# Batch 1's order of work dealt anew in a single-core attention and SwiGLU kernel

## The chip, the core and the metric

The kernel runs on one core of a Trainium2 chip. Its engines run side by side, each through its own list of instructions in order: TensorE (PE in the profile) multiplies matrices, VectorE (DVE) and GpSimd (POOL) do elementwise work, ScalarE (ACT) copies and takes exponentials, SyncE (SP) issues DMA transfers; ACT issues some transfers too. Semaphores make an instruction wait for what it needs. The metric is the device time of the one core in microseconds, start to end, so lower is better.

## What is computed

Eight batches, each of 8 heads with 512 tokens and 32 states of 64 elements. Tokens read from the states and the states read from the tokens, and both results go through one SwiGLU layer with a norm ahead of it:

```python
scores  = softmax(scale * x @ state.T)    ; xread = scores @ state
scores2 = softmax(scale * state @ x.T)    ; sread = scores2 @ x
y  = concat([xread, sread], axis=2)       # (8, 8, 544, 64) -> 4352 rows of 512
xn = y / sqrt(mean(y*y) + 1e-6) * rms_g
g  = xn @ w_gate                          # 512 -> 1536
out = (g * sigmoid(g) * (xn @ w_val)) @ w_out
```

All of it is in float32.

## The kernel before

The weights are converted and stored in DRAM during batch 0. Batches 1 to 7 then run one body each (lines 1288 to 1306), which builds some 17 "streams": Python generators, each of which issues one small step when it is called. A string of letters, written out by hand or by a planner, says whose step comes next. Batch 1 has a string of its own, `FIRST` (line 37), batches 2 to 6 use `PERIOD` and batch 7 uses `LAST`. The schedule is manual: each engine, and each queue of transfers, works in the string's order. A step's data dependencies follow from the program; a buffer that is still in use makes its next owner wait until it is given back.

The streams of batch 1, with the names used below:

- `h`: 42 products on PE (line 806) for six pairs of hidden columns. Pair n has x1, z1, x2, z2, y, x3 and x4, so "h5.z2" is one step. Two products of the next pair come ahead of x4. x, y and z are PSUM banks; x has two buffers, y and z one.
- `t`: per pair three ACT copies out of x, z and x again, and the SiLU (lines 853 to 860). `u`: per pair the DVE sums g1 += z, g0 += y, c += x, then fin1 and fin0 (line 882), which multiply gate and value into the hidden tile `hb`; pairs 3 to 5 have two more (lines 888 and 894).
- `v`, `x`, `w`: folding the states into the gate and value weights. `v` and `w` are products on PE (line 659), called v2 to v5 for this batch and w0, w1 for the next; `x` copies them (ACT, line 671) and forms their four sums (POOL, lines 686 to 689).
- `p`: 49 products on PE (line 1109) in seven groups p0 to p6 of seven steps each ("p3.3" is the fourth step of group 3), the two-level fast multiplication with `w_out`. `k`: the DVE sums that these need. q0.0 to q6.3 (lines 1157 to 1163) are four quarter sums for each group, "half" (line 1168) changes `hb` in place, "add" (line 1149) adds a bank to a kept copy. `c` copies the banks out (ACT, line 1119). `o` stores the output.
- `q`: only in batch 1: the quarter sums of `w_out` on POOL (line 1063), W0 to W6, four steps each, and their store to DRAM (`t_d<-w`, line 1065). `G` and `g` fetch them again from there for each use (`w<-t_d`, line 1055). The tile `w` has three buffers for all of these.
- `f` fetches weights (`w_m<-w_d`, 1 MB each, line 194), `l` loads the state and x of batch 3.
- `a`: what the tokens of batch 2 read: transpose of the states, four transposes `xB` of x, a transfer to DRAM and four back (`xG`, on ACT's queue, lines 378 and 383), the scores (PE, line 403), softmax on DVE and ACT, two transposes into `aT_s` (line 503), the reads (PE, line 530), squares (ACT, line 537), the norm (lines 452 to 469) and the scaling of `aT_s` by it (line 544).
- `s`: what the states of batch 2 read: two maxima, exponentials (line 564), their block transpose `eB` (DVE, line 582), a transfer to DRAM (line 585) and four back into `e` (line 589), both on ACT's queue; then the state read (PE, line 600), which multiplies these transposed exponentials with x, its scaling (line 611), a transpose (line 615) and a copy (line 617).

The lines where the transposed exponentials leave and return:

```python
nc.scalar.dma_start(out=e_d[b % 2].rearrange(...), in_=eB.rearrange(...))
for g in range(4):
    nc.scalar.dma_start(out=e2T[Ns * g:Ns * g + Ns].rearrange(...),
                        in_=e_d[b % 2][:, :, g].rearrange("j t f -> t j f"))
```

Lines 659 to 1005 hold several functions which all write PSUM tiles named `at`, `pv` and `f`: `at` and `pv` have two buffers each.

Of the kernel before, what the change touches and what calls it, by code (L numbers as in the profile page):

```python
# [34 lines left out]
)  # L35

FIRST = (
    "vxhthhthhthuxuufththaaaaaqfhhqthahtqqquuuuxavvhuhhxxtuthuhthtuhuhuaqhvfxxxtuqqqx"
    "tqhqqqqhutkqqhqtaahauhuGGhutuhhhutGuuhtthhhxxuuxtqqquaaauaahhhthagthhthsuuuuuuhp"
    "ppkpptukupuqqqqkkppukkkkkppaakkkggkcacppppppppcappppssaaakplqapkkkkkpkkkppppaaak"  # L40
    "ccaasapppssakscfqaaaapqkkappkkkakppppakkosasqksappppskssgglsaoooapspppakkkaooafw"
    "wxsxxpgcpcowxoxfxg"
)
LAST = (
    "vxhhffththhtuhhhavuttuuhhtfuhhgxxthhhuuuxxtuthuhtthuhuxhutuvxxxvhthhutkxghhtuhut"
# [1299 lines left out]
```

## Time and profile before

| what | us |
|---|---|
| runs | 762.13, 758.90, 762.27 (median 762.13) |
| the profiled execution | 759.87 |
| its span in the trace | 758.1 |
| PE busy in the span | 745.8 (98%) |
| DVE busy | 597.9 (79%) |
| ACT busy | 350.4 (46%) |
| POOL busy | 293.9 (39%) |
| all DMA queues | 146.17 MB, mean 193 GB/s |

The profiled execution's own time is 1.77 us above its span: what lies ahead of the first and behind the last instruction. "Busy" counts time in which the engine had an instruction running. An engine near 100% can still lose time when its instructions run slower than elsewhere, so the stretches of one batch are best compared with those of another that runs the same instructions. Batch 1 runs from about 131 us to 221 us in the trace, batches 2, 3 and 4 follow at about 80 us each.

### The profile page before, as it was taken

What the parts mean: (1) busy time and instruction counts of PE and PEld (TensorE: products, weight loads), DVE (VectorE), ACT (ScalarE), POOL (GpSimd) and SP (SyncE); (2) the same over time, 40 slices, a digit from 0 to 9 for tenths busy, and PEclk for the clock granted to TensorE, in tenths of its full rate; (3) what the DMA queues carried; (4) which work ended last, traced back from release to release, by engine and by line L of the source; (5) the groups of instructions that cost most, each with busy time, mean ns of one, the idle gap of its engine ahead of it and who ended that gap; (6) DMA issues with size and microseconds to landing.
All of it is one profiled execution on the core that took longest, in us unless ns stands there. A gap on an engine that the chain in (4) does not pass through costs nothing.

```text
span 758.1 us, 14411 instructions
## 1 busy us (share of the span) xinstructions
PE 745.8 (98%) x5641; PEld 596.5 (79%) x5641; DVE 597.9 (79%) x1000; ACT 350.4 (46%) x548; POOL 293.9 (39%) x379
## 2 busy tenths in 40 slices
PE   9999999999889999999999999999999999999998
PEld 7633444779768898879877997799788987899997
DVE  4999997679937997689948994799579965787961
ACT  5989883552235522643255425543456236411220
POOL 2000004992574326532465129312842275323600
PEclk9999999999999999999999999999999999999999
DMA  9887945773866176725684477517661866132311
GB/s 297 263 265 264 346 170 181 272 249 112 270 199 236 35 292 201 287 56 196 245 280 115 161 245 244 185 65 301 216 224 26 304 204 216 53 103 108 139 56 29
DMA packets 58787, 146.17 MB, mean 193 GB/s; under 512 B 11616, under 2 KB 29536, under 8 KB 51808
## 3 DMA queue, kind: packets, MB, share of 16 engines
q1 hardware_dynamic: 47152, 125.78, 47.3%
q10 hardware_dynamic: 11568, 19.47, 9.0%
q8 instruction: 45, 0.74, 0.4%
q14 instruction: 22, 0.18, 0.1%
HBM read 116.46 MB, written 28.77 MB: 192 GB/s over the span
## 4 chain that ended last, share of the span: by engine, by line
PE 92%; DVE 6%; DMA 1%; issue 1%; ACT 0%; ACTq 0%; POOL 0%; DVEq 0%; POOLq 0%
PE f L806 38%; PE f L1109 27%; PE f L909 6%; PE pv L702 6%; PE at L659 3%; PE pv L659 3%; PE f L972 2%; PE at L600 1%; PE f L1241 1%; PE at L403 1%; DMA e<-e_d 1%; PE at L530 1%; DVE hb L1168 0%; DVE hb L882 0%; PE at L307 0%
## 5 line engine op out<-in xcount | busy, mean ns | idle before, releaser
L806 PE MATMUL f<-aT_s,v 128*128 128x256 f32 x504 | 119.7, 382 | 0.0
L806 PEld LDWEIGHTS f<-aT_s,v 128*128 128x128 f32 x504 | 94.6, 190 | 24.7 <-issue 8.4
L1135 POOL TENSOR_TENSOR kept<-kept 128x256 f32<-128x256 f32 x28 | 23.1, 824 | 175.4 <-DVE kept L1149 174.2
L1119 ACT COPY kept<-f 128x512 f32<-128x512 f32 (+1 forms) x56 | 29.5, 531 | 131.2 <-PE f L1109 84.4
L869 DVE TENSOR_TENSOR g<-g,f 128x512 f32<-128x512 f32 x84 | 57.5, 687 | 41.2 <-PE f L806 38.5
L806 PE MATMUL f<-aT_t,vs 128*128 128x256 f32 x336 | 87.1, 383 | 0.9 <-ACT g L853 0.8
L1109 PE MATMUL f<-w,h 128*128 128x128 f32 x588 | 74.7, 277 | 0.9 <-DVE h L1159 0.9
L806 PEld LDWEIGHTS f<-aT_t,vs 128*128 128x128 f32 x336 | 62.7, 190 | 15.9 <-POOL vs L686 4.2
L1109 PEld LDWEIGHTS f<-w,h 128*128 128x128 f32 x588 | 69.9, 193 | 6.0 <-issue 4.9
L860 ACT ACTIVATE hb<-g 128x1024 f32<-128x1024 f32 x42 | 44.4, 1058 | 53.4 <-DVE g L869 53.3
L686 POOL TENSOR_TENSOR vs<-v 128x256 f32<-128x256 f32 x42 | 31.7, 754 | 78.7 <-ACT v L671 78.7
L300 POOL TENSOR_TENSOR ri<-ss,mhalf 128x4 f32<-128x4 f32 x8 | 10.7, 1341 | 118.2 <-DVE ss L440 107.0
L858 ACT COPY g<-f 128x512 f32<-128x512 f32 x42 | 24.6, 587 | 45.5 <-PE f L806 45.5
L909 PE MATMUL f<-wo,hb 128*128 128x512 f32 x96 | 44.5, 600 | 0.0
L806 PE MATMUL f<-aT_t,v 128*128 128x256 f32 x168 | 43.5, 382 | 0.8 <-DVE c L869 0.8
L882 DVE TENSOR_TENSOR hb<-hb,f 128x512 f32<-128x512 f32 (+1 forms) x48 | 31.0, 646 | 16.5 <-PE f L806 16.5
L806 PE MATMUL f<-aT_s,vs 128*128 128x256 f32 x168 | 43.8, 383 | 0.0
L702 PE MATMUL pv<-aT_s,v 128*128 128x512 f32 x96 | 43.6, 597 | 0.0
L1109 PE MATMUL f<-wo,h 128*128 128x128 f32 x336 | 42.3, 276 | 0.4 <-DVE h L1161 0.4
L869 DVE TENSOR_TENSOR c<-c,f 128x512 f32<-128x512 f32 (+1 forms) x48 | 31.3, 652 | 13.7 <-PE f L806 13.7
L1109 PE MATMUL f<-wo,hb 128*128 128x128 f32 x336 | 42.1, 275 | 0.0
L882 DVE TENSOR_TENSOR hb<-hb,c 128x512 f32<-128x512 f32 (+1 forms) x48 | 36.6, 763 | 5.9 <-ACT hb L860 5.1
(221 smaller groups left out, 1689.0 us busy)
## 6 DMA issues: line engine op xcount, KB each, us to landing
w_m<-w_d SPq DMA_DIRECT2D x48, 1024.0 KB, 6.1
w<-t_d SPq DMA_DIRECT2D x49, 576.0 KB, 5.4
out_dram<-kept SPq DMA_DIRECT2D x56, 128.0 KB, 1.9
raw<-in_moe_w_val_dram SPq DMA_DIRECT2D x6, 1024.0 KB, 5.3
raw<-in_moe_w_out_dram SPq DMA_DIRECT2D x6, 1024.0 KB, 7.1
w_d<-w_m SPq DMA_DIRECT2D x6, 1024.0 KB, 4.9
x_b<-in_x_dram SPq DMA_DIRECT2D x6, 1024.0 KB, 7.6
x_d<-xB ACTq DMA_DIRECT2D x6, 1024.0 KB, 4.5
```

The costliest lines, as they stand in the source:

```text
L659: TE.matmul(out=pv[e][Ns * j:Ns * j + Ns, :], lhsT=stT_g[b][D * e:D * e + D, j, :], rhs=w[D * e:D * e + D, j].rearrange("p m k f -> p (m k ...
L686: GE.tensor_tensor(out=vs[:, 0], in0=a21, in1=a22, op=ALU.add)
L702: TE.matmul(out=to[0], lhsT=lhs(i, k), rhs=r, start=(i == 0), stop=(i == len(rhs) - 1))
L806: TE.matmul(out=ps[:, i, 0:half], lhsT=l[:, i, :], rhs=r, start=(start and i == 0 and k == 0), stop=(k == len(lhs) - 1), skip_group_check= ...
L858: SE.copy(gates(q)[1], q["x"][:, :, 0:half])
L860: SE.activation(out=hb[:, 2 * mp:2 * mp + 2, 0:n].rearrange("p m (c t) -> p m c t", c=2), in_=q["g"][:, :, :, 0:half], func=ACTF.Silu if s ...
L869: VE.tensor_tensor(out=to, in0=to, in1=q[ps][:, :, 0:half], op=ALU.add)
L882: VE.tensor_tensor(out=part, in0=part, in1=val, op=ALU.mult)
L909: TE.matmul(out=banks[r], lhsT=hb[:, m, P * r:P * r + P], rhs=wo[:, m, :], start=(m == 0), stop=(m == NM - 1))
L1109: TE.matmul(out=to[half][:, slot, :], lhsT=lhs[:, k, :], rhs=rhs[:, k, :], start=(fresh and n in (0, 4) and k == 0), stop=(k == QM - 1), s ...
L1119: SE.copy(k[:, 4 * i:4 * i + 4 - i], banks[name][i])
L1135: GE.tensor_tensor(out=k[:, 1:3], in0=k[:, 0:1].to_broadcast([P, 2, QD]), in1=k[:, 1:3], op=ALU.add)
```

## The change

Only the string `FIRST` changes. It has 338 letters before and after, and each stream has as many steps as before, so the same instructions are issued, in another order:

```diff
 FIRST = (
-    "vxhthhthhthuxuufththaaaaaqfhhqthahtqqquuuuxavvhuhhxxtuthuhthtuhuhuaqhvfxxxtuqqqx"
-    "tqhqqqqhutkqqhqtaahauhuGGhutuhhhutGuuhtthhhxxuuxtqqquaaauaahhhthagthhthsuuuuuuhp"
-    "ppkpptukupuqqqqkkppukkkkkppaakkkggkcacppppppppcappppssaaakplqapkkkkkpkkkppppaaak"
-    "ccaasapppssakscfqaaaapqkkappkkkakppppakkosasqksappppskssgglsaoooapspppakkkaooafw"
-    "wxsxxpgcpcowxoxfxg"
+    "vhqhthxxvfthhthhhuuttuhuuhtaaxqaxxhhqtvuutaqqaaahhxhuutthhhGthhhqqqquuuhuhxxtthu"
+    "ukttkhlvuhuqxaqaaatqhhftqxfxxuuhtqqqqhhtqGhhhkauuuuuthuuaahtatGsqqufhhhhtuuauhuu"
+    "agstukqquphukukkkkpppkaakqcsppqgppppkgkksqqqqapgapapkaaapppppckkskokkkkkcpppcapp"
+    "ppcaaapppppaaaasaaskppkkkpkkkaaakacppkooppppppppkakpapkaapggssapsspkkkpooaawwxco"
+    "xxssssflcoowxxxsfg"
 )
```

Read engine by engine, the orders differ in these places:

| where | before | after |
|---|---|---|
| PE, pair 0 and 1 | v3 and v4 together after h1.y | v3 after h0.x2, v4 after h1.y |
| PE, pair 3 | v5 after h3.x1 | v5 after h3.z2 |
| PE, into the output products | h5.x4, p0.0 | p0.0, h5.x4 |
| PE, group 4 | reads after p4.3 | reads after p4.1 |
| PE, group 6 | p6.0, state read, norm sums, p6.1, transpose of the state read, p6.2 to p6.4, norm rows, w0, p6.5, p6.6, w1 | p6.0 to p6.2, norm sums, p6.3 to p6.6, norm rows, w0, state read, transpose of it, w1 |
| DVE, quarter sums q0 | q0.0 before u3; q0.1 to q0.3 between the last sums of u5 | q0.0, q0.1 before u3, q0.2 inside u3, q0.3 inside u5 |
| DVE, softmax | first maximum of `a` inside u4; q4.1 between the two halves of the last step | first maximum inside u5, before fin1; q4.1 after both halves and after `eB` |
| ACT, pair 5 | both copies of the scores before t5's first copy | one before it, the other after t5's third copy |
| ACT, exponentials of `s` | after c.p5's first copy | the first after c.p1's first copy, the second after c.p1's second |
| ACT, four `xG` transfers | one after t2's third copy, three after t3's third copy | all four after t3's third copy |
| ACT, `eB` to DRAM | before c.p5's second copy and the four squares | after three of the four squares |
| POOL | W0 ahead of the sums for v2; last step of W5 and W6 spread over p0 to p5 | W0.0, sums for v2, then the rest; W5 and W6 in one run ahead of the add for p1 |
| SP, fetch G0 | after the store of W3 | after the store of W0 |
| SP, weights w12, w13 | before the store of W0, before the store of W1 | both after the store of W2 |
| SP, weights w14 | after fetch 5 of the quarters | after the store of W4, ahead of fetch 3 |
| SP, state of batch 3 | after fetch 5 of the quarters | after the store of W1 |
| SP, x of batch 3 | after fetch 7, behind the state read | after the fetch of w15, behind the state read |

Fetch 1 and fetch 2 of the quarters stand ahead of the store of W4 in both orders.

## The prediction

> **What bounds the kernel now.** I began with the table by stretches, comparing batch 1 (from its h0.x1 to that of batch 2) with the next two, which issue the same 664 matmul records. Columns: length, busy us of the engines with counts, granted PE clock, DMA share, GB/s.
>
> ```profile
> 131.33:221.43 90.10, 83.90 (x664) 69.98 (x663) 69.18 (x116) 33.60 (x58) 59.59 (x66) 0.98 0.68 221
> 223.46:303.79 80.33, 80.33 (x664) 68.19 (x663) 64.54 (x115) 35.15 (x59) 35.73 (x48) 1.00 0.55 187
> 303.79:383.95 80.16, 80.16 (x664) 68.25 (x663) 64.56 (x115) 35.15 (x59) 34.78 (x46) 1.00 0.59 199
> ```
>
> The other batches are PE without a hole. Batch 1 costs 90.1 - 80.3 = 9.8 us more, and nothing that this change does can bring back more than that. The waits of PE in that stretch (who waited for whom, total, times, longest) say where 6.2 of it is:
>
> ```profile
> PE at L600 <- DMA e<-e_d: 3.3, 1, 3.3
> PE f L1109 <- DVE h L1159: 0.9, 1, 0.9
> PE f L806 <- ACT g L853: 0.8, 1, 0.8
> PE f L806 <- DVE c L869: 0.8, 1, 0.8
> PE f L1109 <- DVE h L1161: 0.4, 1, 0.4
> ```
>
> The rest is 83.90 - 80.33 = 3.6 us of PE running slower. Two-microsecond stretches around the largest wait show why:
>
> ```profile
> 208.00:210.00 2.00, 0.00 (x0) 0.00 (x0) 1.66 (x3) 0.00 (x0) 1.47 (x2) 1.00 0.69 267
> 212.00:214.00 2.00, 2.00 (x10) 2.00 (x11) 1.86 (x8) 0.00 (x0) 0.96 (x1) 0.50 0.38 71
> 214.00:216.00 2.00, 2.00 (x15) 2.00 (x14) 0.73 (x2) 0.00 (x0) 1.86 (x3) 0.70 0.89 259
> ```
>
> PE idles 3.3 us, then its clock is 0.50 and 0.70. The chain of waits for this place (start, length, what) runs:
>
> ```profile
> 196.49 0.73 DVE eS L500
> 197.25 0.72 DVE aT_s L503
> 198.07 1.26 DVE eB L582
> 199.34 1.37 DMA e_d<-eB
> 200.71 1.48 ACT sq L537 x3
> ...
> 203.43 7.05 DMA e<-e_d
> 210.62 1.10 PE at L600 x64
> ```
>
> So the state read stood in PE's list when its transposed exponentials were still under way; of the four transfers the last took 7.1 us, the first three 3.2 to 3.7, while fetches 6 and 7 of the quarters, issued at 203.5 and 203.9 on SP's queue, took 6.8 and 7.6. Before that, from 161 to 208 us, DVE hardly pauses, and the chain runs through it: there it sets the pace, PE is near.
>
> **What the Trainium skill says.** "TensorE: Matmul & The Clock Gate", section "What's actually happening": an idle window of about 3.4 us puts PE back to half clock. The trace agrees: 3.29 us idle, then 0.50. "DMA: Bandwidth & Descriptors", section "Queues, rings and completion order": SP's and ACT's queues are rings on the same 16 engines, served in turn by packets. The 7.1 us against 3.2 beside two fetches of 576 KB fit. "GPSIMD Engine Reference", section "1. Specifications": POOL shares SBUF interfaces with DVE when that reads two inputs. The W sums of one shape take 1.0 us at 135 to 150 us and 1.46 at 162 and 169 us, where DVE is busy.
>
> **The change, part by part.** Prices from the trace: h product 0.87, v or w product 1.02 (0.86 behind another), p step 0.67, reads 1.04 (batch 2's, 283.49 to 284.53), state read 1.03; DVE 0.60 for 128x512, 0.47 for 128x384, "half" 0.87, eB 1.24, a divide pair 0.2 + 0.25 (here often 0.8 + 0.25).
>
> *Pairs 0 to 5.* Same PE work. I laid every product of the new order end to end from 131.33 us and asked for each what it needs. v3 now starts at 133.9; its weights were issued at 122.3 and took 7.0 (129.3). v4 starts at 142.9, w10 landed by 137.2. x1.3's first copy frees the `at` tile for the states' transpose at about 140.7, wanted at 141.0. q0.0, q0.1 between u2 and u3 fill a DVE gap (2.16 us before u2.fin0 until now): u3.g1 can start at 155.4 anyway. POOL's sums for v3, v4, v5 end by about 146, 154 and 164; h3.z1, h4.z1, h5.z1 come at 151.7, 158.8, 165.9. The second copy of the scores no longer stands ahead of t5, so the 0.82 wait on L853 goes. The two later landings on this path are the `xG` transfers. All four go out at about 155.0 to 156.8 (three did at 155.8 to 157.1) and the scores start at 164.1. Those three took 3.9 to 6.3 us: 163 at the latest. Beside them are now the store of W2 and, once POOL is through W2 (155.5 to 157), two fetches of 1 MB; they hide or not. I take no wait; the bounds are 0 and 4. h5.z2 then ends at 169.5 (170.9 before), u5.g1 starts at 169.7 (171.13).
>
> *From u5.g1, called 0, to the reads.* DVE does 0.5 us less before q3.1 than now (out: q0.1, q0.2 at 0.47 each; in: the first maximum, 0.60). PE: h5.y, h5.x3 and p0.0 end at 2.15; h5.x4 needs c += x at 2.35 (0.2 lost), where p0.0 has eaten most of the 0.8. p0.4 would start at 5.2 and needs the second x buffer from u5.fin0, at 5.8: 0.6 lost. p1, p2, p3.0 to p3.2 end at 19.3. The copy c.p1.1 has slipped behind two exponentials on ACT: maximum and subtraction end at 14.0, exponential 14.7, copy 15.3, wanted by p2.4 at 15.2: 0.1. p3.3 needs q3.1 at 20.0: 0.7 (0.9 now). p4.0, p4.1 end at 24.0, and the reads, moved up by two steps, need the second `aT_s` transpose: 20.0 plus q3.2, q3.3, q4.0 (1.4), multiply and transpose (1.4), sum 0.6, divide pair 1.0, multiply and transpose 1.5 makes 25.9. So 1.9 lost, the largest new wait. Now the reads begin at 26.06 and are stretched to 1.87, so the absolute delay is no greater.
>
> *Reads to the end.* p4.3 to p4.6 wait for q4.1, now behind eB: 27.7. p4 ends at 30.6, p5 35.3. The `eB` transfer goes out at about 29, the four returns at 32, landed by 39 even at 7.1 us; the state read comes at 41.9. The 3.3 us wait and the slow clock behind it go, since no single wait in my list exceeds 1.9. Norm sums follow p6.2 at 37.3, p6 ends at 40.4, norm rows 40.8, w0 41.8, state read 42.9. Late next is the transpose of the state read: the reciprocal stands behind the scaling of `aT_s` (1.2), so PE waits from 42.9 to 43.9 (1.0), then w1 waits 0.3 for the copy that frees its `at` tile. w1 ends at 45.3, v2 of batch 2 at 46.2, and its h0.x1 starts. POOL: power 38.6 to 40.0, the add for u2 to 43.0, four sums for batch 2's tokens to 46.0, first sum for its weights 46.8; h0.z1 wants that at 47.1.
>
> *Transfers of W.* Fetch 2 still waits for p0.4 to free a buffer; W4's store follows it, then 1 MB of w14 (new), then fetch 3. 2.2 MB at some 350 GB/s is 6.3 us; fetch 3 should land at 185 to 186.5 and p3.2 is at 188. W6 starts when p3.4 frees a buffer, fetch 6 lands near 204, p6.2 is at 206.4. x of batch 3 is issued at 213 and took 6 to 8; its first transpose is near 226. Those are hidden.
>
> *Sum.* Batch 2's h0.x1 at 169.7 + 46.2 = 215.9 against 221.43: 5.5 us. Each of the steps with under 0.3 us of slack can add a little; I take 0.5 off and keep 5.0. Batch 2 and later are unchanged. The profiled execution was 759.87 (span 758.1 + 1.77), so 754.9. It lies 2.26 below the median of 762.13; taken off the median it is 757.1. I predict 757.2.
>
> **The rivals.**
> - Half kept: DVE paces this part, and the waits on it grow where the hole was (each of reads, p3.3, p0.4 half a microsecond longer, the transpose likewise): 5.0 - 2.5, so 759.6. For it: DVE at 69 of 90 us busy and idle hardly at all from 161 to 208. Against: its list is 0.5 us shorter up to q3.1.
> - More won: the small waits overlap and only 1.5 us over 80.3 stays: 90.1 - 81.8 = 8.3, 753.8. For it: batch 2's similar order runs without a hole. Against: batch 2 has no 28 sums of W and other places for q4.1.
> - Slower: `xG` is late at the scores. W2's store, w12, w13 and `xG` are 3.6 MB; at 350 GB/s 10.5 us from 155.2, or, as one weight fetch did at 143 to 145 us, 11.3 from the last issue: landing 168.1, 4.0 after the scores want it. PE then idles over 3 us, and the slow clock returns at its price of 3.6 (83.90 - 80.33). 4.0 + 3.6 - 5.0 = 2.6 lost: 764.7. It decides from a wait of about 3 us. For it: those 11.3 and a DMA share of 1.04 at 160 to 165. Against: `xG` goes first by up to 2 us and the queues are served in turn, so it should have half of the engines.
> - No slack bought at all is excluded by the order: the returns have some 3 us, and PE has other work there.
>
> **How the numbers follow.** Forecast 0.54, half kept 0.20, more won 0.11, slower 0.15. This kernel's runs spread over 3.4 us, so 0.5% (3.8 us) is about what can be told from no change. The forecast's own range is 754.5 to 760; with the others 753 to 763.5, leaving out a tenth at each end. Faster (below 758.3): 0.43 of the forecast's 0.54, all of more won and 0.04 of half kept, 0.58. Slower (above 765.9): the worse part of the slow rival and a little beyond, 0.13. Same: 0.29.
>
> **What would show it.** Right: batch 1 takes 84 to 85.5 us; no wait of L600 on `e<-e_d`; clock 1.00 throughout; waits of L530 on L503 of 1 to 2 us, of L1109 on L1159 below 1, of L615 on L611 near 1. Wrong: a wait of L403 on `xG`, of L1109 on `w<-t_d`, or a clock of 0.5 anywhere after 131 us; a later start of u5.g1 than 170 says that the pairs were misjudged; waits at the reads above 2.5 say that DVE's list was.

## The result, and the profile after

| | before | after |
|---|---|---|
| median of 6 runs, us | 761.25 (758.90 to 762.87) | 765.97 (762.91 to 766.05) |
| the profiled execution, us | 759.87 | 762.91 |
| its span in the trace, us | 758.1 | 761.1 |

After stands to before as 1.0054, with a 95% interval of 1.0029 to 1.0079: 0.5% slower, where 757.2 us had been forecast. It is the "Slower" rival that came in. It had been priced at 2.6 us lost (764.7); 4.7 were lost by the medians, 4.1 by the ratio and 3.0 in the two profiled executions.

The table by stretches, of the profile after: batch 1, batch 2, and four stretches of 2 us. Columns: stretch, length, busy us of PE, PEld, DVE, ACT and POOL with counts, granted PE clock, DMA share, GB/s.

```profile
131.22:224.59 93.37, 86.15 (x664) 69.30 (x663) 70.62 (x116) 33.42 (x58) 58.99 (x66) 0.98 0.62 206
166.00:168.00 2.00, 0.00 (x0) 0.00 (x0) 1.20 (x1) 0.00 (x0) 2.00 (x2) 1.00 1.02 295
168.00:170.00 2.00, 0.03 (x4) 0.06 (x6) 0.00 (x0) 0.00 (x0) 1.92 (x3) 1.00 0.84 315
170.00:172.00 2.00, 2.00 (x15) 0.43 (x16) 0.18 (x1) 0.00 (x0) 1.92 (x3) 0.55 0.10 39
172.00:174.00 2.00, 2.00 (x6) 1.61 (x7) 1.95 (x4) 0.73 (x2) 0.10 (x1) 0.60 0.82 276
224.59:304.80 80.21, 80.21 (x663) 68.25 (x664) 64.85 (x115) 35.20 (x59) 35.08 (x47) 1.00 0.58 195
```

Batch 2 is as full as before, so the whole loss lies in batch 1: 93.4 us against 90.1. There is still a hole with a slow clock behind it, but in another place, at 165 us where it was at 207: PE does nothing from 166 to 170 while the DMA engines are full or nearly so (1.02 and 0.84), and then runs at 0.55 and 0.60.

The waits of PE in batch 1, after (who waited for whom: total us, times, longest):

```profile
PE at L403 <- DMA xG<-x_d: 4.2, 1, 4.2
PE at L530 <- DVE aT_s L503: 1.0, 1, 1.0
PE at L615 <- DVE sr L611: 0.7, 1, 0.7
PE f L1109 <- ACT kept L1119: 0.4, 1, 0.4
PE f L1109 <- DVE h L1159: 0.3, 1, 0.3
PE f L1109 <- DVE hb L882: 0.3, 1, 0.3
```

The wait of L600 on `e<-e_d` is gone. A wait of the scores (L403) on `xG` has come. PE's timeline at that place (start, length, operation, and in brackets the idle time before it with its releaser):

```profile
162.87 1.89 PE L806 MATMUL f<-aT_s,v 128*128 128x256 f32 x8
164.69 1.04 PE L403 MATMUL at<-xG,stT 64*32 64x512 f32 x2
169.97 1.82 PE L403 MATMUL at<-xG,stT 64*32 64x512 f32 x14 [4.24 <-DMA xG<-x_d]
```

Two of the 16 matmuls ran; the other 14 start 5.3 us after the first two had. The bracket counts 4.24, from the modelled end of the second. What held them is in the chain of waits (start, length, what; its `issue` pieces of up to 0.14 us are left out here), and in the timelines of the two issuing queues, ACT's and SP's:

```profile
155.40 1.10 ACTq L383
156.53 0.98 ACTq L383
157.54 12.29 DMA xG<-x_d
169.97 1.82 PE at L403 x14
171.79 7.17 PE f L806 x28
```

```profile
155.01 3.04 ACTq L383 DMA_DIRECT2D xG<-x_d  x4
155.39 0.34 SPq L1065 DMA_DIRECT2D t_d<-w  x1
155.83 1.72 SPq L194 DMA_DIRECT2D w_m<-w_d  x2
```

All in the same 3 us: four `xG` transfers of 256 KB on ACT's queue, and on SP's the store of W2 (576 KB) and w12 and w13 (1 MB each). The four landed after 3.1, 9.0, 12.2 and 12.3 us (w12 and w13 after 9.9 and 13.0), against 3.9 to 6.3 for the three that before issued here.

### The profile page after: what moved, and what is told of

Its sections match the earlier page's. It is cut to its first block, busy times and chain, and to the rows that moved or that the text cites. A ratio compares the mean times of both kernels' runs of the same rounds, so it can differ in the third digit from the quotient of the medians.

```text
span 761.1 us, 14420 instructions
## 1 busy us (share of the span) xinstructions
PE 747.7 (98%) x5641; PEld 595.6 (78%) x5641; DVE 599.7 (79%) x1000; ACT 350.4 (46%) x548; POOL 293.2 (39%) x379
## 4 chain that ended last, share of the span: by engine, by line
PE 92%; DVE 5%; DMA 2%; issue 1%; ACTq 0%; ACT 0%; POOL 0%; DVEq 0%; POOLq 0%
PE f L806 37%; PE f L1109 28%; PE f L909 6%; PE pv L702 5%; PE at L659 3%; PE pv L659 3%; PE f L972 2%; DMA xG<-x_d 2%; PE at L403 1%; PE at L600 1%; PE f L1241 1%; PE at L530 1%; DVE hb L1168 0%; PE at L307 0%; DVE eS L500 0%
```

## The experiments

Ratios are to the kernel before on the same chip, with 95% intervals; times are medians. Two theories stood at first. **Crowd**: w12 and w13 beside `xG` make the loss; without them the change is a gain. **Late**: the order itself makes `xG` late or brings little.

**e1: w12 and w13 ahead of the crowd.** w12 goes right after w11 and w13 after fetch G0:

```diff
-    "vhqhthxxvfthhth...hhhGthhhqqqq..." "...qxaqaaatqhhftqxfxxuuht..."
+    "vhqhthxxvffthhth...hhhGfthhhqqqq..." "...qxaqaaatqhhtqxxxuuht..."
```

> The kernel after with only the two 1 MB weight fetches (w12, w13) put back ahead of the store of W1; the order is otherwise that of after. Crowd (the two fetches hold up the xG transfers): xG lands within 7 us of its issue, no wait at L403, clock 1.00 after 131 us, about 757.5 us, 5 below before or more. Late (xG is late since all four go out together at 155 us, crowd or no crowd): the wait at L403 stays at 3 to 5 us and the time at 764 to 766. Elsewhere (the rest of the new order costs as much as the wait): no wait at L403, yet 761 or more.

Measured: 757.5, ratio 0.9957 (0.9944 to 0.997). No wait at L403, clock 1.00 behind it, batch 1 took 88.9 us. It isn't a clean undoing, though: w13 now lay beside `x_d<-xB`, which took 11.7 us to land, so that `xG` itself was issued later, at 158.7 (some 3 us later within the batch), and still landed in time.

**e2: the same crowd put into the kernel before.** w12 and w13 behind the store of W2, nothing else changed.

```diff
-    "...aaaaaqfhhqtha...uhuaqhvfxxxtuqqqx" "tqhqqqqhutk..."
+    "...aaaaaqhhqtha...uhuaqhvxxxtuqqqxtq" "hqqffqqhutk..."
```

> The kernel before with only w12 and w13 moved behind the store of W2. Crowd: three xG transfers go out beside 2 MB as in after, PE waits 3 to 5 us at L403 and the clock falls, so 765 to 769 us (before 761.3). Late: one of the four xG still goes out early, so no wait at L403 and 760 to 762.

Measured: 763.45, ratio 1.0034 (1.0015 to 1.0054): slower, but less than Crowd asked. PE's largest two waits in its profile:

```profile
PE at L600 <- DMA e<-e_d: 3.3, 1, 3.3
PE at L403 <- issue: 2.0, 1, 2.0
```

The old hole stays and a second one comes at the scores. The profile puts it down to "issue", but the last `xG`, issued at 156.7, landed after 10.6 us, at 167.3, and the rest of the scores starts at 167.37, so it is the same wait; the clock behind it was 0.56. In this order one of the four `xG` is away by 148.6 us, before the fetches, which is the likely reason for the smaller hole.

**e3: the named part of the change alone.** In the kernel before, the state read and its scaling go behind w0, the transpose and copy behind p6.5, and x of batch 3 behind w15:

```diff
-    "...psksappppskssgglsaoooapspppakkkaooafw" "wxsxxpgcpcowxoxfxg"
+    "...psksappppsksggaoooappppakkkaooaflwwss" "xxxpssgcpcowxoxfxg"
```

> The kernel before with only the end dealt anew: state read after w0, its transpose after p6.5, and the load of x of batch 3 behind the fetch of w15. My ledger: the 3.3 us wait at L600 and the slow clock behind it go, the end then hangs on POOL's norm chain: 755 to 757 us. If the 7 us transfer was not the end of it (another wait stands right behind, such as fetch 6 of the quarters or the norm): 759 to 761.

Measured: 757.82, ratio 0.996 (0.9948 to 0.9972). The wait on `e<-e_d` went, and the largest of PE's waits became others, the first ahead of the clock's fall to 0.50 at 212 to 214 us:

```profile
PE f L1109 <- DMA w<-t_d: 1.7, 1, 1.7
PE f L1109 <- DVE h L1159: 0.9, 1, 0.9
```

So moving the state read does bring a gain by itself. The slow clock left in this profile isn't the rule: the profiled execution took 759.29, and 13 of the 20 runs, with a mean granted clock of 0.999 or more, took 756.8 to 758.1.

**e4: `xG` sooner.** The kernel after, with the four `xG` ahead of t3's third copy; w12 and w13 stay where the change put them.

```diff
-    "ukttkhlvuhuqxaqaaatqhhftqx..."
+    "uktaaaatkhlvuhuqxqtqhhftqx..."
```

> The kernel after with the four xG transfers issued ahead of t3's third copy, about 1.2 us sooner, ahead of the 2 MB of weights. Crowd: their 1 MB is mostly through before the fetches start, so the wait at L403 falls from 4.2 us to below 2 and the clock stays up: 757 to 761 us. Late: 1.2 us less wait, 764 to 765.

Measured: 758.0, ratio 0.9962 (0.9951 to 0.9973). The four were issued at 153.4 to 154.8, some 1.6 to 2.7 us earlier each, and landed after 3.3 to 6.4 us. No wait at L403.

**e9: only w12 and w13 back behind the store of W3.** The cleanest undoing of the cause, two letters of the string:

```diff
-    "...atqhhftqxfxxuuhtqqqqhhtqGhhhk..."
+    "...atqhhtqxxxuuhtqqqffqhhtqGhhhk..."
```

> The kernel after with only w12 and w13 moved behind the store of W3 (two letters), so that neither the xG transfers nor the one that feeds them has the 2 MB beside it. Crowd: no wait at L403, clock 1.00 behind it, batch 1 in 87 to 88 us, 757.5 to 758.5 in all, the same as with xG sooner (758.0). If the crowd only moves on to fetch 1 of the quarters: a wait of L1109 on w<-t_d and 760 or more. If something else in the new order held xG up: wait as in after, 765 or more.

Measured: 757.61, ratio 0.9954 (0.9941 to 0.9966). `xG` goes out as in after; here is ACT's queue, and then PE at the scores:

```profile
155.16 2.67 ACTq L383 DMA_DIRECT2D xG<-x_d  x4
...
164.85 1.09 PE L403 MATMUL at<-xG,stT 64*32 64x512 f32 x16
```

All 16 matmuls run without a break: the transfers landed 3.3 to 6.4 us after their issue. Batch 1 and batch 2 in the table:

```profile
131.31:218.66 87.35, 83.43 (x671) 68.30 (x663) 70.88 (x116) 33.20 (x58) 60.74 (x66) 1.00 0.66 220
218.66:298.87 80.21, 80.21 (x670) 68.25 (x663) 64.83 (x115) 35.17 (x59) 35.07 (x47) 1.00 0.57 196
```

From the position of two fetches alone the time goes from 1.0054 to 0.9954 of before.

The kernel before has quick runs of its own, however. Of the 23 beside e9, the three with a mean granted clock of 0.999 or more took 757.2 to 758.7, and the nine with 0.996 or less took 761.0 to 764.7. So the larger part of what e9 wins over before goes with a clock that no longer drops; against those three runs, which are few, it is about 1 us.

**e5: what the slow clock costs.** The kernel after, with ten more products, of the identity with itself, on PE ahead of batch 2's scores. They fill most of the hole (the trace counts them as 20), and nothing uses their result:

```diff
+            if b == 2:
+                warm = vps.tile([P, 4, P], F32, name="pv")
+                for _ in range(10):
+                    TE.matmul(out=warm[:, 0:2], lhsT=ident, rhs=ident.unsqueeze(1).to_broadcast([P, 2, P]), ...)
```

> The kernel after with ten matmuls of the identity (128x256, into a free pv buffer that nobody reads) ahead of the scores of batch 2, so that PE works through 4.3 us of its wait for xG. It computes the same output. If the slow clock behind the wait has a price of its own (about 2 us: the scores and the next two products at half speed): xG lands as late as in after, clock 1.00 behind it, and the time falls by 1.5 to 2.5 us to about 764. If the clock costs nothing (DVE, which also waits for the scores, sets the pace there): same as after, 766.

Measured: 762.35, ratio 1.0011 (0.9999 to 1.0023). PE at the place, then two stretches of the table:

```profile
164.90 4.48 PE L403 MATMUL pv<-ident 128*128 128x256 f32 x20
169.31 1.04 PE L408 MATMUL at<-xG,stT 64*32 64x512 f32 x2
171.38 1.09 PE L408 MATMUL at<-xG,stT 64*32 64x512 f32 x14 [1.02 <-DMA xG<-x_d]
```

```profile
170.00:172.00 2.00, 0.98 (x15) 0.21 (x14) 0.00 (x0) 0.00 (x0) 1.92 (x3) 1.00 0.42 166
172.00:174.00 2.00, 2.00 (x19) 1.44 (x8) 1.42 (x3) 0.72 (x2) 0.45 (x1) 1.00 0.22 39
```

`xG` is as late as ever (171.4), but the clock is 1.00 behind it. In the profiles, from the second part of the scores to u5.g1 takes 177.09 - 171.38 = 5.7 us here and 177.33 - 169.97 = 7.4 in after: 1.7 for the clock there. Over the runs it is 765.97 - 762.35 = 3.6 (3.3 by the ratios), more than was expected. Two stretches of the table, laid from the start of the slow clock to its end, the first in before and the second in after, show why the two can differ:

```profile
211.77:215.18 3.41, 3.41 (x17) 3.41 (x18) 2.81 (x9) 0.00 (x0) 2.10 (x2) 0.50 0.48 111
170.19:173.61 3.42, 3.42 (x19) 1.53 (x6) 1.74 (x3) 0.59 (x1) 1.91 (x2) 0.50 0.39 123
```

In each profile the clock was at 0.50 for 3.4 us, which costs half of that, 1.7. But the profiled execution of after was the quickest of its six, with a mean granted clock of 0.997, where the others show 0.995 and 0.996. Of a span of 764.2, 0.005 is 3.8 us, about two such stays. As wholes the two profiled executions took the same, 762.91 in after and 762.97 here, mainly since here `xG` landed 1.1 us later within the batch.

**e6: is it the size of the packets?** The weights' rows are longer than the 2 KB rows of `xG`. In the kernel after, w12 and w13 were each fetched as two transfers of 2 KB pieces.

```diff
-            nc.sync.dma_start(out=new_w(n), in_=w_d[n % (NM // 2)])
+            w, d = new_w(n), w_d[n % (NM // 2)]
+            for r in range(2) if n in (12, 13) else ():
+                nc.sync.dma_start(out=w[:, r::2], in_=d[:, r::2])
...
```

> The kernel after with w12 and w13 each fetched in two transfers whose runs are 2 KB long (every second of four parts) in place of one with runs of 8 KB; bytes and place in the queue as in after. If the queues are served in turn by packet and the larger packets of the weights starve the 2 KB rows of xG: xG now gets about half, its last transfer lands within 8 us of its issue, the wait at L403 falls below 2 us, 758 to 761 us. If xG waits for the bytes, not the packets: landing and wait as in after, 765 to 767.

Measured: 760.49, ratio 0.9991 (0.9975 to 1.0007). Inconclusive: the time lies where smaller packets were to bring it, the landing (9.2 us after the last issue) doesn't. ACT now took 4.8 us over the four issues instead of 3.0, so the last `xG` left at 159.8 and landed at 169.0, near the 169.8 of after; small waits for ACT put the scores off to 166.0, PE then waited 2.0 us and the clock stayed at 1.00. What was won is mainly the clock. The DMA view shows what the shorter rows did to the shares. In after, from 160 to 167 us with both queues at work, SP's moved 230 packets with 1.75 MB and ACT's 237 with 0.43: one for one, and 20% of the bytes for `xG`. In e6, from 163 to 168 us with the engines full, the packets were alike, and yet it was 552 with 1.06 MB against 200 with 0.35: 25%. So packets of unequal size in equal turns describe after, but the turns weren't equal in e6, for a reason that stays open.

**e7: half the crowd.** Of the two fetches only w12 goes early, as in e1.

```diff
-    "vhqhthxxvfthhth..." "...qxaqaaatqhhftqxfxxuuht..."
+    "vhqhthxxvffthhth..." "...qxaqaaatqhhtqxfxxuuht..."
```

> The kernel after with only w12 put back to its early place, w13 left behind the store of W2. Crowd: 1 MB less beside xG, at some 300 GB/s 3.4 us, so xG's last transfer lands 8 to 9 us after its issue and the wait at L403 is 0.5 to 1.5 us, clock 1.00: 757 to 760. If any fetch behind W2's store is enough: wait above 3 us, 763 or more.

Measured: 762.14 with 20 runs from 757.84 to 765.53, ratio 1.0004 (0.9988 to 1.0021); the expectation of 757 to 760 was missed. The profiled execution was the longest of the 20. PE there, and the stretch behind it:

```profile
168.05 1.23 PE L403 MATMUL at<-xG,stT 64*32 64x512 f32 x2 [2.87 <-DMA xG<-x_d]
169.65 1.95 PE L403 MATMUL at<-xG,stT 64*32 64x512 f32 x14 [0.37 <-DMA xG<-x_d]
```

```profile
170.00:172.00 2.00, 2.00 (x15) 0.47 (x2) 0.33 (x1) 0.00 (x0) 1.92 (x3) 0.50 0.10 16
```

One fetch of 1 MB is enough to hold `xG` up in some executions. Here the bytes alone don't explain it: from 164 to 168 us all queues together moved 133 GB/s, less than half of what they reach when full, and the last `xG` still landed at 169.5. Why it was so slow is open. The mean granted clock of the runs goes with their time: the seven at 0.999 and above took 757.8 to 761.0, the thirteen at or below 0.998 took 761.2 to 765.5. In this profile it was at 0.50 from 168.7 to 175.6 us, and again from 206.3 to 209.7. That the hole in the other runs lies near the length at which the clock drops is likely, but was not seen.

**e8: everything together.** After with `xG` sooner, w12 and w13 behind the store of W3, the reads after p4.2, the copy c.p1.1 ahead of the second exponential of `a`, and p6.6 between the state read and its transpose.

```diff
-    "ukttkhlvuhuqxaqaaatqhhftqxfxxuuhtqqqqhhtqG..." "...apgapapkaaappppp" "ckkskok..."
+    "uktaaaatkhlvuhuqxqtqhhtqxxxuuhtqqqffqhhtqG..." "...apgapcapkaaappppp" "kkskok..."
-    "ppcaaapppppaaaasaaskppk..." "...sapsspkkkpooaawwxco" "xxssssflc..."
+    "ppcaaapppppaapaasaaskpk..." "...sapsspkkkooaawwxcox" "xsspssflc..."
```

> A version against both: after, with the four xG ahead of t3's third copy, w12 and w13 behind the store of W3, reads after p4.2, c.p1's second copy ahead of a's second exponential, and p6.6 between the state read and its transpose. My ledger: e4 less 0.4 at p2.4, 0.6 at the reads, 0.4 at the end: 756 to 757. If DVE sets the pace anyway, no better than e4: 758. If w12 and w13 now hold up fetch 1 of the quarters: a wait of L1109 on w<-t_d and 759 or more.

Measured: 757.12 (4 runs), ratio 0.9942 (0.9922 to 0.9961). It beats both kernels, but isn't to be told from e9, whose interval it overlaps. Its waits of PE show why the last three moves brought nothing to speak of:

```profile
PE f L1109 <- DVE h L1159: 2.0, 2, 1.1
PE f L806 <- POOL w L1063: 0.5, 1, 0.5
PE at L530 <- DVE aT_s L503: 0.4, 1, 0.4
```

The waits at the reads (1.0) and at the transpose (0.7) shrink or go, and PE waits 2.0 for DVE's quarter sums instead, against 0.3 in after and 1.2 in e9. That fits with DVE setting the pace here, whatever the place at which PE waits.

**e10: the crowd of after, whole, in the kernel before.** As e2, with the fourth `xG` moved to the other three.

```diff
-    "...aaaaaqfhhqtha...uhuaqhvfxxxtuqqqx" "tqhqqqqhutkqqhqtaahauhu..."
+    "...aaaaaqhhqtha...uhuqhvxxxtuqqqxtqh" "qqffqqhutkqqhqtaaahauhu..."
```

> The kernel before with after's pattern of transfers around the scores and nothing else of the change: w12 and w13 behind the store of W2, and all four xG after t3's third copy. Crowd: the wait at L403 appears here too, 3 to 5 us, with the clock at about 0.5 behind it, on top of the wait at L600: 766 to 771 us. If the wait in after came from its other orders (v3, v5, the late xB): less than 2 us of wait and 762 to 764, as in e2.

Measured: 772.05, ratio 1.0166 (1.0123 to 1.021): slower by more than foretold, and elsewhere. A part of the chain of waits:

```profile
156.43 9.06 DMA w_m<-w_d
165.49 0.02 issue
165.51 0.31 ACTq L383
165.82 0.05 issue
165.86 0.04 ACT hb L860
```

The fourth `xG` wasn't issued until w12 had landed, and ACT's copies stood behind it, on which PE waited 7.9 us; that it was w12's landing which released ACT is the profile's inference. Nothing of that is seen in after, where no issue took over 1.1 us. So this run shows how dear the meeting of these transfers can be, though its third `xG`, issued at 156.6, did land only after 10.8 us; it doesn't show the wait of after again. Why that issue waited for another queue's transfer was not pursued.

## Why the prediction was wrong

**The step that failed** is in "Pairs 0 to 5", at the `xG` transfers: "I take no wait; the bounds are 0 and 4." Measured: a start 5.3 us later than the first two matmuls (4.24 in the bracket), and behind it the slow clock. It rested on two sentences. The first, "Those three took 3.9 to 6.3 us: 163 at the latest", took a duration from a place without the fetches to one with 2 MB of them; they took up to 12.3. The second, in the rival, was "it should have half of the engines". For the 12.3 us behind the last issue, the three late transfers moved 768 KB: 64 GB/s of the 315 that all moved from 157.5 to 169.8, 20%. The Trainium skill ("DMA: Bandwidth & Descriptors", section "Queues, rings and completion order") says that the engines take turns between queues by whole packets. It promises turns, not halves of the bytes, and I read it as the latter. The packet counts under e6 agree with turns in after, 230 against 237, and show how little they are worth in bytes.

The rival's landing at 168.1 (measured 169.8) came from the 11.3 us that one weight fetch had taken elsewhere in before's trace, counted from the last issue; it should have been the forecast. Its sum of bytes, 10.5 us from 155.2, gives 165.7, which is 4 us too early. That its 2.6 us of loss came near the 3.0 of the profiles was luck: the wait was right (4.0 foretold, 4.2 in the bracket), but the clock was put 1.9 too high and the gain 2.1 too high, and the two cancel.

**The price of the slow clock** was misread. 83.90 - 80.33 = 3.6 was taken for the clock alone, but the clock was at 0.50 for 3.41 us in that profile, which is 1.7, and in e9, where it is 1.00 throughout, PE is still busy for 83.43 us in batch 1 against 80.21 in batch 2. "Busy" holds waits too: the modelled end of a group's first matmuls reaches into the wait behind them, as at the scores (1.04 us for two matmuls in after, 1.09 for all 16 in e9). The 3.6 between the medians of after and e5 is another thing, some two stays in place of one. What held was the link between an idle stretch and the clock, from "TensorE: Matmul & The Clock Gate", section "What's actually happening", for a hole of 4 to 5 us. The same section says that the window in which idleness is counted runs freely, so that the point shifts from run to run. The runs agree near the limit: a hole of 2.0 us in the bracket (3.0 from start to start) was followed by 0.56 in e2 and by 1.00 in e6, and e7's twenty runs fall on either side. "It decides from a wait of about 3 us" should have been a band.

**The gain without the hole** was put at 5.0 us and is 2.9 (spans of 758.1 before and 755.2 in e9), or 3.1 by the medians of e9's comparison. The terms, from e9's trace: u5.g1 was to start at 169.7 and starts at 171.3. Of these 1.6, 0.75 is there at the scores already (164.1 foretold, 164.85), and 0.5 is a wait of one of pair 5's products, which the profile puts down to a sum of W on POOL; ahead of it a multiply of DVE (line 882) took 1.47 us beside those sums, where 0.60 had been taken. From u5.g1 to batch 2's h0.x1 46.2 were foretold and 47.35 taken (47.2 in after). Those 1.15 have all arisen by the reads: the rest of them starts 27.0 us after u5.g1 (198.35), 25.9 foretold, and 20.3 follow, as foretold. On the way p3.3 started at 20.7, where DVE's q3.1 had been expected at 20.0, and DVE was busy for 32.2 of the 33 us from 172 to 205. So DVE's list, on which both wait, was some 1.1 us longer than the ledger had it. That is the reason which the "Half kept" rival gave, and its size (5.0 - 2.5) is near too, but 1.6 of the missing 2.75 lie ahead of the part that it spoke of. The single waits are no proof of it: 1.0 in the bracket at the reads (2.1 from start to start, 1.9 foretold), 0.7 at the transpose (1.0) and 1.2 at p3.3 (0.7). Two rivals thus held together, and the likeliest case was the one that neither touched.

**What was right**: the wait of L600 and the slow clock at that place are gone (the four returns took 2.5 to 4.6 us in all batches of after), e3 shows that moving the state read is worth 0.4% alone, no fetch of W is late, and batch 2 runs on unchanged at 80.2 us.

So the loss is a gain and a larger new cost. In the profiles the gain is 2.9 us (758.1 to 755.2 in e9) and the cost 5.9 (755.2 to 761.1), of which 1.7 is the clock and 4.2 the hole. Over the runs the gain is 3 us or so, and the hole with its clock costs about 8 (0.9954 to 1.0054 of before is 7.6).

## What to carry to other kernels

When a transfer is moved, look at what is issued beside it on all queues until the moment it is needed, and don't count on a share of the engines. Their bytes, divided by the rate that the trace shows for full engines, say how early it can be through if it comes last; here it was later still (3.7 MB at 315 GB/s from 155.2 is 167, landed 169.8; in e7's profile 2.7 MB from 155.4 would be 164, landed 169.5). The longest landing that the trace of before showed for a single fetch, 11.3 us, was the better guide. In after, a transfer with 7 us between its issue and its use came 5 us late beside two fetches which nobody needed yet, and either 1.6 to 2.7 us of an earlier issue or a later place for those fetches cured it. A hole that is closed in one place is worth its whole price only if the engine next in line (here DVE) has room, and other transfers that are moved in the same change can open a new one, slow clock included, so look for it upstream too. And compare runs by their granted clock as well as by their medians: one profile may hold one slow stay where the usual run holds two.

## What the runs showed that was not expected

- ACT's issues took longer while SP issued too: the four of `xG` took 0.35 to 1.10 us each, 3.0 together, beside SP's three (after), 4.8 beside five of SP's (e6), and 1.8 when SP was quiet (e4).
- An issue seems able to wait for a transfer of another queue: ACT stood for 9.6 us, until SP's w12 had landed (e10, as the profile infers it).
- The clock fell to 0.50 for 3.41 or 3.42 us at a time in before, after and e2, and for 6.83 in e7, twice that.
- One kernel with a hole that comes and goes spreads over 7.7 us (e7), where the kernel after without that hole (e9) spreads over 2.0.
